# A hand-written order for the first batch's two halves in a Nyström attention and two-layer gated kernel

## The chip, the core and the metric

The kernel runs on one core of a Trainium2 chip. The metric is the device time of one execution in microseconds (us). A core has TensorE (matrix products into PSUM), VectorE, ScalarE, GpSimd and the queues that start DMA transfers; here nearly all transfers are issued from the SyncE queue (SP). In the profile's rows the engines are called PE (matmuls), PEld (its weight loads), DVE (VectorE), ACT (ScalarE), POOL (GpSimd) and SP. Each engine works through its own list of instructions in order and waits at an instruction until what it needs is there.

## The reference

Four batches of eight heads go through a Nyström attention with 32 landmarks, and the result through two gated layers. Only the first part is touched by the change:

```python
def _attn_ref(q, k, v):                       # 4 x 8 x 576 x 64
    q_lm = q.reshape(B, H, 32, 18, D).mean(axis=3)
    k_lm = k.reshape(B, H, 32, 18, D).mean(axis=3)
    A  = softmax(q    @ k_lm.T / 8)           # own scores
    Bm = softmax(q_lm @ k_lm.T / 8)
    C  = softmax(q_lm @ k.T    / 8)
    Z = Bm.T / (norm1(Bm) * norminf(Bm) + 1e-6)
    for _ in range(6):
        Z = 2 * Z - Z @ Bm @ Z
    return A @ Z @ C @ v
...
x = moe(x, silu gate); return moe2(x, sigmoid gate)   # 2304 x 512, inner width 1536
```

## The kernel before

A batch's eight heads are worked on in two halves of four heads (g = 0 and 1); names end in batch and half, so `kin0_1` holds the keys of batch 0, second half. `front(b, g)` does a half: `lm_steps("k")`, then `lm_steps("q")`, each of which sums 18 tokens into a landmark (`lm`, `ls`), transposes the landmarks (`lt`) and writes them masked into `bdk` or `bdq` on ScalarE, and turns the tokens by nine transposes in three groups (`tp`), copied by ScalarE into `kq`. Then come the landmark scores `cs` (maxima `cmx`, `nmx` on VectorE, exponentials `e` on ScalarE with their sums `csm`), the small landmark matrix `bm`, the transposed weights `et` and `eT`, their product with the values (`cv`, into `bc`), and the half's own scores `as` with maxima `amx` and exponentials `sx`. For the very first half the sum is one `tensor_reduce` and a copy on VectorE, for all other halves six additions on GpSimd (line 145 on).

`back(b)` takes both halves: it normalises `bs`, iterates the inverse in seven small products `nw`, each followed by an update `rw` on VectorE, and transposes the result to `ut` (lines 345 and 346). Between the rounds `a_steps` normalises, transposes and splits the own scores into `AH`; in batch 0 every round also issues some `warm` matmuls that compute nothing. `uw_steps` then multiplies `ut` with the first layer's weights (`pu`); the big products `pg`, `pv`, `po` follow.

Weights arrive as 64-bit floats in `raw` tiles (three of them) and are converted by `convert`: two ScalarE steps (lines 372 and 375), then two VectorE steps (377 and 381), results in `w1`, or `cv1` for the output weights, whose high and low parts `wo` are split off behind (408 on ScalarE, 409 on VectorE).

The order: the code records its work in a certain order; a scheduler below it sets each engine's list from that, and may move an instruction ahead of others where nothing forbids it. `tc.issue_after` (in the helper `behind`) holds an instruction behind a named one on its engine's list. Before the loop over words ("B0 I0 F10 U00 ...") the two halves of batch 0 run as generators that stop at the words "keys" and "weights": first half up to its weights, second half's keys, rest of the first, rest of the second. SP issues keys, queries and values of the first half, then keys and queries of the second, then a mix of later inputs and weights as buffers come free.

Of the kernel before, what the change touches and what calls it, by code (L numbers as in the profile page):

```python
# [7 lines left out]
F32 = mybir.dt.float32  # L8
# [8 lines left out]
def nystrom_moe_kernel(tc, q, k, v, wg1, wv1, wo1, wg2, wv2, wo2, out):  # L17
    nc = tc.nc
    B, H, S, D = q.shape
    M = 32  # L20
# [60 lines left out]
    def behind(what):  # L81
        return tc.issue_after(order[what].ins) if what in order else nullcontext()

    def load_attn(b, which, g):
        if which == "v":
            t = att.tile([TP, 4, R, D], F32, tag="vin", name=f"vin{b}_{g}", bufs=1)
            nc.sync.dma_start(t, v[b, 4 * g:4 * g + 4].rearrange("h (p r) d -> p h r d", r=R))
# [32 lines left out]
    def pst(b, shape, nm, g=0):  # L120

        tag = "n" if nm in ("nw", "ut") else "a"
        if b == 0:
            tag = {"tp": "gv", "cs": "o", "as": "o"}.get(nm, tag)
        return ptile(shape, tag, f"{nm}_{b}_{g}")

    def front(b, g):

        nm_ = f"{b}_{g}"

        def sm(tag, shape, bufs=2):
            return small(tag, shape, nm_, bufs)

        def lm_steps(which):
            src = inq[which, b, g]
            if (b, g) == (0, 0):
                if which == "k":
                    order["lm"] = sm("ls", [P, NU, D], 1)
                lm = order["lm"][:, 0:2] if which == "k" else order["lm"][:, 2:4]
            else:  # L140
                lm = sm("lm", [P, 2, D], 1)

            if (b, g) > (0, 0):
                x = sm("ls", [P, NU, D], 1)
                nc.gpsimd.tensor_tensor(x, src[:, 0:NU], src[:, NU:], op=ALU.add)
                nc.gpsimd.tensor_tensor(x[:, 0:4], x[:, 0:4], x[:, 4:8], op=ALU.add)
                nc.gpsimd.tensor_tensor(x[:, 0:2], x[:, 0:2], x[:, 2:4], op=ALU.add)
                nc.gpsimd.tensor_tensor(x[:, 0], x[:, 0], x[:, 8], op=ALU.add)
                for w in range(2):
                    nc.gpsimd.tensor_tensor(lm[:, w], x[:, 0], x[:, 1], op=ALU.add)  # L150
# [3 lines left out]
            yield  # L154
            bdt = sm("bd" + which, [P, 2, P], 1)

            def landmarks():
                ps = pst(b, [P, P], "lt", g)
                with behind(("tp", b, g, which)):
                    order["lt", b, g, which] = nc.tensor.transpose(ps, flat(lm), ident)  # L160
                for w in range(2):
                    nc.scalar.activation(bdt[:, w], ps, AF.Copy, scale=pmask[:, w:w + 1])


            tokens_first = (b, g) == (0, 0) or (b, g, which) == (0, 1, "k")
            if not tokens_first:
                landmarks()
                yield
            t = sm("kq", [P, NU, P])
            for i in range(3):  # L170
                ps = pst(b, [P, 3, P], "tp", g)
                for j in range(3):
                    u = 3 * i + j
                    with behind("scores" if (b, g, which) == (0, 1, "k") else None):
                        order["tp", b, g, which] = nc.tensor.transpose(ps[:, j], flat(src[:, 2 * u:2 * u + 2]), ident)  # L175
                nc.scalar.copy(t[:, 3 * i:3 * i + 3], ps)
                yield
            if tokens_first:
                landmarks()
                yield  # L180
            load_next(b, g, which)
            return bdt, t
# [833 lines left out]
```

## Time and profile before

| | us |
|---|---|
| median of three runs | 860.38 (860.14 to 862.11) |
| the profiled execution | 859.69 |
| its span in the profile | 857.9 |
| TensorE busy | 838.2 |
| VectorE busy | 661.9 |
| end of `ut`, which releases the first big product | 42.11 |

The profile is of one execution. Times in its rows count from the span's start. "Busy" of TensorE contains waits inside the pipeline. The number in brackets at the end of a row is the time that the engine stood idle just before, with what ended it.

### The profile page before, as it was taken

What the parts mean: (1) busy time and instruction counts of PE and PEld (TensorE: products, weight loads), DVE (VectorE), ACT (ScalarE), POOL (GpSimd) and SP (SyncE); (2) the same over time, 40 slices, a digit from 0 to 9 for tenths busy, and PEclk for the clock granted to TensorE, in tenths of its full rate; (3) what the DMA queues carried; (4) which work ended last, traced back from release to release, by engine and by line L of the source; (5) the groups of instructions that cost most, each with busy time, mean ns of one, the idle gap of its engine ahead of it and who ended that gap; (6) DMA issues with size and microseconds to landing.
All of it is one profiled execution on the core that took longest, in us unless ns stands there. A gap on an engine that the chain in (4) does not pass through costs nothing.

```text
span 857.9 us, 15969 instructions
## 1 busy us (share of the span) xinstructions
PE 838.2 (98%) x6214; PEld 698.8 (81%) x6214; DVE 661.9 (77%) x1298; ACT 471.0 (55%) x965; POOL 59.3 (7%) x90
## 2 busy tenths in 40 slices
PE   6899999999999999999999999999999999999997
PEld 4677777888888888889898888888888788888886
DVE  5999676866976987577889777979779985678655
ACT  5677565456652754235359655555637485455421
POOL 5634330000000000000000000000000000000000
PEclk9999999999999999999999999999999999999999
DMA  8775421021430631002117515244334552232003
GB/s 277 196 230 175 126 57 29 2 87 48 145 117 1 194 102 50 1 26 74 37 62 239 179 58 188 99 148 159 111 140 164 166 179 88 74 123 74 7 19 99
DMA packets 41677, 93.32 MB, mean 109 GB/s; under 512 B 5889, under 2 KB 9217, under 8 KB 41601
## 3 DMA queue, kind: packets, MB, share of 16 engines
q1 hardware_dynamic: 40352, 90.72, 33.1%
q10 hardware_dynamic: 1248, 1.57, 0.7%
q8 instruction: 49, 0.80, 0.4%
q14 instruction: 28, 0.22, 0.1%
HBM read 72.88 MB, written 19.40 MB: 108 GB/s over the span
## 4 chain that ended last, share of the span: by engine, by line
PE 91%; DVE 4%; ACT 2%; DMA 1%; issue 1%; POOL 0%; SPq 0%; ACTq 0%; DVEq 0%; POOLq 0%
PE po L65 36%; PE pv L65 22%; PE pg L65 22%; PE pu L65 3%; PE pvr L65 2%; PE pgr L65 2%; PE nw L65 1%; PE tp L175 1%; PE cs L65 1%; DMA kin<-in_k_dram 1%; PE as L65 1%; DVE cv L377 1%; PE et L232 1%; PE cv L65 0%; DVE AH L273 0%
## 5 line engine op out<-in xcount | busy, mean ns | idle before, releaser
L65 PE MATMUL po<-wo,h 128*128 128x512 f32 (+1 forms) x435 | 109.7, 388 | 0.0
L65 PEld LDWEIGHTS po<-h,wo 128*128 128x128 f32 x480 | 82.3, 188 | 27.9 <-issue 7.5
L65 PE MATMUL po<-h,wo 128*128 128x512 f32 (+1 forms) x480 | 103.9, 373 | 0.0
L65 PE MATMUL pg<-AH,uw 128*128 128x288 f32 x552 | 94.4, 298 | 0.6 <-ACT uw L408 0.6
L65 PEld LDWEIGHTS po<-wo,h 128*128 128x128 f32 x435 | 81.1, 188 | 16.9 <-ACT h L408 0.3
L65 PE MATMUL pv<-AH,uw 128*128 128x288 f32 x552 | 92.1, 298 | 0.9 <-DVE sg L590 0.6
L835 DVE TENSOR_TENSOR oacc<-po,oacc 128x512 f32<-128x512 f32 (+1 forms) x91 | 60.2, 678 | 34.8 <-PE po L65 34.7
L65 PEld LDWEIGHTS pg<-AH,uw 128*128 128x128 f32 x552 | 80.0, 188 | 7.1 <-issue 3.4
L65 PEld LDWEIGHTS pv<-AH,uw 128*128 128x128 f32 x552 | 78.7, 188 | 4.5 <-DVE sg L590 2.3
L372 ACT ACTIVATE cv<-raw 128x512 f32<-128x512 f32 x84 | 56.9, 679 | 28.7 <-DVE st L381 9.0
L65 PE MATMUL po<-hl,wo 128*128 128x288 f32 x384 | 66.9, 309 | 0.1
L377 DVE SCALAR_TENSOR_TENSOR cv<-cv,cv 128x512 uint32<-128x512 uint32 x84 | 59.0, 705 | 1.4 <-ACT cv L375 1.3
L65 PEld LDWEIGHTS po<-hl,wo 128*128 128x128 f32 x384 | 54.0, 188 | 6.9 <-issue 3.3
L375 ACT ACTIVATE cv<-raw 128x512 uint32<-128x512 uint32 x84 | 55.9, 673 | 5.0 <-DVE wo L409 5.0
L648 DVE TENSOR_TENSOR acc<-po,acc 128x512 f32<-128x512 f32 x64 | 43.5, 686 | 14.9 <-PE po L65 14.9
L65 PE MATMUL pg<-AH,wk 128*128 128x512 f32 x192 | 52.1, 390 | 0.0
L65 PE MATMUL pv<-AH,wk 128*128 128x512 f32 x192 | 51.5, 389 | 0.0
L593 ACT ACTIVATE sg<-pg 128x288 f32<-128x288 f32 x64 | 26.0, 406 | 42.7 <-PE pg L65 42.5
L408 ACT CAST h<-h 128x288 fp32r<-128x288 f32 x64 | 27.4, 430 | 30.5 <-DVE h L594 30.3
L409 DVE TENSOR_TENSOR h<-h,h 128x288 fp32r<-128x288 f32 x64 | 29.1, 456 | 19.0 <-ACT h L408 18.8
L65 PEld LDWEIGHTS pv<-AH,wk 128*128 128x128 f32 x192 | 36.0, 188 | 7.5
L65 PEld LDWEIGHTS pg<-AH,wk 128*128 128x128 f32 x192 | 35.7, 188 | 7.2
(208 smaller groups left out, 1721.5 us busy)
## 6 DMA issues: line engine op xcount, KB each, us to landing
raw<-in_moe_w_out_dram SPq DMA_DIRECT2D x36, 512.0 KB, 4.5
raw<-in_moe_w_gate_dram SPq DMA_DIRECT2D x48, 128.0 KB, 3.4
raw<-in_moe_w_val_dram SPq DMA_DIRECT2D x48, 128.0 KB, 3.5
raw<-in_moe_w_gate_dram SPq DMA_DIRECT2D x24, 256.0 KB, 3.0
raw<-in_moe_w_val_dram SPq DMA_DIRECT2D x24, 256.0 KB, 4.0
wkd<-st SPq DMA_DIRECT2D x24, 256.0 KB, 3.0
wtd<-tf SPq DMA_DIRECT2D x12, 512.0 KB, 3.0
st<-wkd SPq DMA_DIRECT2D x24, 256.0 KB, 3.1
```

The costliest lines, as they stand in the source:

```text
L65: return nc.tensor.matmul(o, l, r, start=start, stop=stop, skip_group_check=True)
L175: order["tp", b, g, which] = nc.tensor.transpose(ps[:, j], flat(src[:, 2 * u:2 * u + 2]), ident)
L232: nc.tensor.transpose(ps[:, j, :], flat(e[:, r // 2, r % 2]), ident)
L372: nc.scalar.activation(t0, hiw.bitcast(F32), AF.Copy, scale=2.0 ** -112)
L375: nc.scalar.activation(u1, low, AF.Copy, scale=0.875 * 2.0 ** -29, bias=0.49)
L377: nc.vector.scalar_tensor_tensor(u1, u0, 3, u1, op0=ALU.logical_shift_left, op1=ALU.bitwise_or)
L408: nc.scalar.copy(hi, x)
L409: nc.vector.tensor_tensor(lo, x, hi.bitcast(F32), op=ALU.subtract)
L593: nc.scalar.activation(sg, pss[0], AF.Silu)
L648: nc.vector.tensor_tensor(sl, ps, sl, op=ALU.add)
L835: nc.vector.tensor_tensor(acc[:, ds], ps, acc[:, ds], op=ALU.add)
```

## The change

The generators of batch 0 are replaced by a class `Front` with a method for each step and a function `first_fronts` that calls the steps of both halves in an order written out by hand. All other batches run the same steps from `Front.steps`.

- Queries are loaded ahead of keys. For the first half the query landmarks come first, then key tokens, key landmarks' sum, landmark scores, then the query tokens.
- Three of the four landmark sums of batch 0 (queries and keys of the first half, keys of the second) are five additions each on VectorE; the second half's queries stay on GpSimd.
- The first half's own scores are recorded ahead of the second half's key tokens, whose transposes are held behind them, and whose copies are held behind the exponential of `bs`.
- The weights' first two pieces are loaded ahead of the second batch's keys (`load_to(2)`), the third behind the second half's values.
- The query transposes of batch 1, half 0, are held behind the second, their landmarks behind the third round of batch 0's inverse.
- The first two ScalarE steps of the first weight piece are held behind a copy of the second half's keys.

```diff
+        def sums(self, which, eng, after=None):
+            src = inq[which, self.b, self.g]
...
+                x = self.sm("sx", [P, NU, D], 3)
+                lm = x[:, 4:6]
+            with behind(after):
+                eng.tensor_tensor(x, src[:, 0:NU], src[:, NU:], op=ALU.add)
+            eng.tensor_tensor(x[:, 0:4], x[:, 0:4], x[:, 4:8], op=ALU.add)
+            eng.tensor_tensor(x[:, 0:2], x[:, 0:2], x[:, 2:4], op=ALU.add)
+            eng.tensor_tensor(x[:, 0], x[:, 0], x[:, 8], op=ALU.add)
...
+                eng.tensor_tensor(lm, x[:, 0:1].to_broadcast([P, 2, D]), x[:, 1:2].to_broadcast([P, 2, D]), op=ALU.add)
...
-                nc.vector.tensor_reduce(lm[:, 0], src.rearrange("p u d -> p d u"), axis=AX.X, op=ALU.add)
-                nc.vector.tensor_copy(lm[:, 1], lm[:, 0])
...
+            with behind(("round", 3) if (self.b, self.g, which) == (1, 0, "q") else None):
+                nc.tensor.transpose(ps, flat(self.lm[which]), ident)
...
+    def first_fronts():
+
+        f, s = Front(0, 0), Front(0, 1)
+        load_to(2)
+        f.sums("q", nc.vector)
+        f.landmarks("q")
+        for i in range(3):
+            f.tokens("k", i)
+        f.sums("k", nc.vector)
+        for w in range(2):
+            f.scores(w)
+        f.landmarks("k")
+        for i in range(3):
+            f.tokens("q", i)
+        f.exponentials()
+        f.norm()
+        load_next(0, 0, "k")
+        s.sums("q", nc.gpsimd)
+        for i0, i1 in ((0, 5), (5, NU)):
+            f.own(i0, i1)
+        s.sums("k", nc.vector, ("shifted", 0, 0))
+        for i in range(3):
+            s.tokens("k", i, ("own", 0, 0), ("bs", 0, 0))
+        f.recip()
+        for hf in range(2):
+            f.turned(hf)
+        f.weighted()
+        load_next(0, 0, "v")
+        s.landmarks("q")
+        for w in range(2):
+            s.scores(w)
+        s.landmarks("k")
+        s.norm()
+        s.exponentials()
+        with behind(("v", 0, 1)):
+            load_to(3)
+            load_next(0, 0, "q")
+            load_next(0, 1, "k")
+        for i in range(3):
+            s.tokens("q", i)
+        load_next(0, 1, "q")
+        s.recip()
+        for hf in range(2):
+            s.turned(hf)
+        s.weighted()
+        for i0, i1 in ((0, 5), (5, NU)):
+            s.own(i0, i1)
...
-        for x in "kqv" if g == 0 else "kq":
+        for x in "qkv" if g == 0 else "qk":
             load_attn(0, x, g)
...
-    fronts = [front(0, g) for g in range(2)]
-    for g, to in ((0, "weights"), (1, "keys"), (0, None), (1, None)):
-        for said in fronts[g]:
-            if to is not None and said == to:
-                break
+    first_fronts()
...
+        if w == "I0":
+            load_next(0, 1, "v")
```

How this moves instructions on the engines' lists shows at three places. In the rows, `x0_1_331` is a tile of batch 0, half 1, with a serial number at the end, and the last figures are the output's size.

VectorE, from the first half's own scores to the second half's first maximum, before:

```order
L254 TENSOR_REDUCE amx0_0_255<-as_0_0_256 128x10
L255 TENSOR_TENSOR sx0_0_254<-as_0_0_256,amx0_0_255 128x320
L254 TENSOR_REDUCE amx0_0_255<-as_0_0_280 128x8
L255 TENSOR_TENSOR sx0_0_254<-as_0_0_280,amx0_0_255 128x256
L263 TENSOR_REDUCE asm0_0_494<-sx0_0_254 128x18
L240 TENSOR_SCALAR bc0_152<-cv_0_0_226,rc0_0_181 128x64
L264 TENSOR_SCALAR asm0_0_494<-asm0_0_494 128x18
L265 RECIPROCAL asm0_0_494<-asm0_0_494 128x18
L201 TENSOR_REDUCE cmx0_1_331<-cs_0_1_335 128x1
L267 TENSOR_TENSOR sx0_0_254<-sx0_0_254,asm0_0_494 128x576
L201 TENSOR_REDUCE cmx0_1_331<-cs_0_1_341 128x1
```

The same place after the change:

```order
L254 TENSOR_REDUCE amx0_0_205<-as0_0_0_206 128x10
L220 TENSOR_SCALAR rc0_0_272<-csm0_0_177 128x1
L255 TENSOR_TENSOR sx0_0_204<-as0_0_0_206,amx0_0_205 128x320
L254 TENSOR_REDUCE amx0_0_205<-as_0_0_230 128x8
L151 TENSOR_TENSOR sx0_1_250<-kin0_1_97 128x576
L255 TENSOR_TENSOR sx0_0_204<-as_0_0_230,amx0_0_205 128x256
L152 TENSOR_TENSOR sx0_1_250<-sx0_1_250 128x256
L221 RECIPROCAL rc0_0_272<-rc0_0_272 128x1
L372 TENSOR_SCALAR bsm0_183<-bsm0_183 128x1
L153 TENSOR_TENSOR sx0_1_250<-sx0_1_250 128x128
L154 TENSOR_TENSOR sx0_1_250<-sx0_1_250 128x64
L341 TENSOR_REDUCE asm0_0_512<-sx0_0_204 128x18
```

The sums of the second half's keys (`sx0_1_250`) now stand between the own scores' steps, and `rc0_0` ahead of them.

VectorE, the last rounds of batch 0's inverse up to the copy of `ut`, before:

```order
L336 SCALAR_TENSOR_TENSOR rw0_540<-rw0_523,nw_0_0_529 128x192
L381 SCALAR_TENSOR_TENSOR w1_0_584<-cv0_620,cv1_621 128x512
L273 TENSOR_TENSOR AH_88<-sx0_1t_580,AH_88 128x576
L336 SCALAR_TENSOR_TENSOR rw0_557<-rw0_540,nw_0_0_546 128x192
L201 TENSOR_REDUCE cmx1_0_708<-cs_1_0_712 128x1
L377 SCALAR_TENSOR_TENSOR cv1_629<-cv0_628,cv1_629 128x512
L342 SCALAR_TENSOR_TENSOR rw0_571<-rw0_557,nw_0_0_560 128x128
L381 SCALAR_TENSOR_TENSOR w1_0_584<-cv0_628,cv1_629 128x512
L346 COPY ut0_84<-ut_0_0_573 128x128
```

The same place after the change:

```order
L418 SCALAR_TENSOR_TENSOR rw0_527<-rw0_510,nw_0_0_516 128x192
L418 SCALAR_TENSOR_TENSOR rw0_541<-rw0_527,nw_0_0_530 128x192
L461 SCALAR_TENSOR_TENSOR cv1_632<-cv0_631,cv1_632 128x512
L418 SCALAR_TENSOR_TENSOR rw0_558<-rw0_541,nw_0_0_547 128x192
L465 SCALAR_TENSOR_TENSOR w1_0_602<-cv0_631,cv1_632 128x512
L461 SCALAR_TENSOR_TENSOR cv1_643<-cv0_642,cv1_643 128x512
L418 SCALAR_TENSOR_TENSOR rw0_575<-rw0_558,nw_0_0_564 128x192
L465 SCALAR_TENSOR_TENSOR cv1_643<-cv0_642,cv1_643 128x512
L424 SCALAR_TENSOR_TENSOR rw0_589<-rw0_575,nw_0_0_578 128x128
L493 TENSOR_TENSOR wo0_0_603<-cv1_643,wo0_0_603 128x512
L428 COPY ut0_84<-ut_0_0_591 128x128
```

Two conversion steps and a low part of the output weights (`cv1_643`, `wo0_0`) now stand ahead of `ut`, the maximum `cmx1_0` behind it, and two rounds follow each other directly. From nmx of the second half to the row ahead of `ut`, the list has 45 instructions before and 47 after.

TensorE, around `ut`, before:

```order
L65 MATMUL cs_1_0_712<-kq1_0_656,bdq1_0_682 32x288
L65 MATMUL nw_0_0_546<-rw0_540 32x96 x8
L65 MATMUL warm0_447<-ident_75 128x128 x2
L65 MATMUL cs_1_0_712<-kq1_0_656,bdq1_0_682 32x288 x3
L65 MATMUL cs_1_0_718<-kq1_0_656,bdq1_0_682 32x288
L65 MATMUL nw_0_0_560<-rw0_557 32x96 x8
L65 MATMUL warm0_447<-ident_75 128x128 x2
L65 MATMUL cs_1_0_718<-kq1_0_656,bdq1_0_682 32x288 x3
L345 MATMUL ut_0_0_573<-ident_75,rw0_571 128x128
L65 MATMUL warm0_447<-ident_75 128x128 x4
L65 MATMUL pu0_0_1_825<-w1_0_584,ut0_84 32x512
```

The same place after the change:

```order
L65 MATMUL nw_0_0_578<-rw0_575 32x96 x8
L65 MATMUL warm0_465<-ident_75 128x128 x2
L65 MATMUL cs_1_0_711<-kq1_0_661,bdq1_0_687 32x288
L427 MATMUL ut_0_0_591<-ident_75,rw0_589 128x128
L65 MATMUL warm0_465<-ident_75 128x128 x4
L65 MATMUL pu0_0_1_830<-w1_0_602,ut0_84 32x512
...
L65 MATMUL cs_1_0_711<-kq1_0_661,bdq1_0_687 32x288 x3
L65 MATMUL cs_1_0_717<-kq1_0_661,bdq1_0_687 32x288 x4
```

Seven of the eight landmark score products of batch 1, half 0, have moved from ahead of `ut` to behind `pu` (eight `pu` rows, of which one stands here).

## Rows read from the trace of the kernel before

**Rows 1.** The page's part 1: busy us, share of span, instructions, by engine.
```profile
PE 838.2 (98%) x6214; PEld 698.8 (81%) x6214; DVE 661.9 (77%) x1298; ACT 471.0 (55%) x965; POOL 59.3 (7%) x90
```

**Rows 2.** Stretches: length, busy us of PE, PEld, DVE, ACT, POOL; clock, DMA, GB/s.
```profile
20.00:25.00 5.00, 2.61 (x36) 1.74 (x28) 4.93 (x13) 2.96 (x10) 4.61 (x7) 0.77 1.01 285
...
30.00:35.00 5.00, 4.38 (x71) 3.52 (x61) 5.00 (x10) 3.10 (x9) 4.69 (x6) 1.00 1.04 259
...
45.00:60.00 15.00, 13.96 (x207) 12.01 (x207) 14.58 (x30) 12.20 (x32) 6.32 (x9) 1.00 0.68 204
...
72.00:80.00 8.00, 6.89 (x108) 4.63 (x105) 7.85 (x16) 4.14 (x10) 4.19 (x6) 1.00 0.44 136
...
120.00:857.00 737.00, 733.23 (x4590) 617.55 (x4580) 564.83 (x1057) 392.36 (x763) 8.93 (x14) 1.00 0.30 96
```

**Rows 3.** VectorE in time, 4 to 43: start, length, line, operation, [idle before].
```profile
4.61 2.14 DVE L152 TENSOR_REDUCE ls<-kin 128x64 f32<-128x1152 f32 x1 [3.53 <-DMA kin<-in_k_dram]
6.78 0.19 DVE L153 COPY ls<-ls 128x64 f32<-128x64 f32 x1
...
13.56 0.21 DVE L223 TENSOR_SCALAR rc<-csm 128x1 f32<-128x1 f32 x1 [1.33 <-ACT e L208]
...
17.00 0.42 DVE L254 TENSOR_REDUCE amx<-as 128x8 f32<-128x256 f32 x1
...
18.41 0.75 DVE L263 TENSOR_REDUCE asm<-sx 128x18 f32<-128x576 f32 x1 [0.53 <-ACT sx L257]
...
21.64 0.21 DVE L206 TENSOR_SCALAR nmx<-cmx 128x1 f32<-128x1 f32 x1
...
41.82 0.29 DVE L346 COPY ut<-ut 128x128 f32<-128x128 f32 x1 [0.38 <-PE ut L345]
42.02 0.45 DVE L201 TENSOR_REDUCE cmx<-cs 128x1 f32<-128x288 f32 x1
42.39 0.68 DVE L377 SCALAR_TENSOR_TENSOR cv<-cv,cv 128x512 uint32<-128x512 uint32 x1
```

**Rows 4.** TensorE in time, 4 to 24 us, same columns.
```profile
4.72 2.15 PE L175 MATMUL tp<-ident,kin 128*128 128x128 f32 x9 [4.72 <-DMA kin<-in_k_dram]
...
10.12 1.18 PE L65 MATMUL cs<-kq,bdq 128*32 128x288 f32 x16 [0.47 <-ACT bdq L162]
...
11.29 1.20 PE L175 MATMUL tp<-ident,kin 128*128 128x128 f32 x9
...
19.06 1.18 PE L65 MATMUL cs<-kq,bdq 128*32 128x288 f32 x16
...
22.69 0.45 PE L232 MATMUL et<-ident,e 128*96 128x128 f32 x1 [2.39 <-ACT e L208]
```

**Rows 5.** ScalarE in time, 8 to 45 us.
```profile
12.31 0.65 ACT L208 ACTIVATE e<-cs,nmx 128x288 f32<-128x288 f32 x1
...
13.63 0.86 ACT L176 COPY kq<-tp 128x384 f32<-128x384 f32 x2
...
17.60 0.78 ACT L257 ACTIVATE sx<-sx 128x320 f32<-128x320 f32 x2
...
19.87 0.71 ACT L372 ACTIVATE cv<-raw 128x512 f32<-128x512 f32 x1
```

**Rows 6.** VectorE in time, 20 to 34 us: operations with two operands in SBUF.
```profile
20.20 1.04 DVE L267 TENSOR_TENSOR sx<-sx,asm 128x576 f32<-128x576 f32 x1
...
22.67 1.78 DVE L381 SCALAR_TENSOR_TENSOR w<-cv,cv 128x512 uint32<-128x512 uint32 x1
...
33.38 0.74 DVE L267 TENSOR_TENSOR sx<-sx,asm 128x576 f32<-128x576 f32 x1
```

**Rows 7.** GpSimd in time: the first addition of a landmark sum.
```profile
10.07 1.42 POOL L145 TENSOR_TENSOR ls<-kin 128x576 f32<-128x576 f32 x1 [8.77 <-DMA kin<-in_k_dram]
...
22.16 1.74 POOL L145 TENSOR_TENSOR ls<-qin 128x576 f32<-128x576 f32 x1
```

**Rows 8.** TensorE in time, 33 to 42 us: one product of a round.
```profile
33.61 0.53 PE L65 MATMUL nw<-rw 32*32 32x96 f32 x16
```

More of the change, by code (lines that the diff above doesn't have):

```diff
@@ L149, in lm_steps @@
                 for w in range(2):
-                    nc.gpsimd.tensor_tensor(lm[:, w], x[:, 0], x[:, 1], op=ALU.add)
+                    eng.tensor_tensor(lm[:, w], x[:, 0], x[:, 1], op=ALU.add)
             else:
-                nc.vector.tensor_reduce(lm[:, 0], src.rearrange("p u d -> p d u"), axis=AX.X, op=ALU.add)
-                nc.vector.tensor_copy(lm[:, 1], lm[:, 0])
[L154 to L162, printed above, removed]
@@ L165, in lm_steps @@
[L165 to L177, printed above, removed]
@@ new lines, in tokens @@
+        def tokens(self, which, i, after=None, copy_after=None):
+            src = inq[which, self.b, self.g]
+            if i == 0:
+                self.t[which] = self.sm("kq", [P, NU, P])
+            ps = self.psum([P, 3, P], "tp")
+            for j in range(3):
+                u = 3 * i + j
+                with behind(after):
+                    nc.tensor.transpose(ps[:, j], flat(src[:, 2 * u:2 * u + 2]), ident)
+            with behind(copy_after):
+                order["copy", self.b, self.g, which] = nc.scalar.copy(self.t[which][:, 3 * i:3 * i + 3], ps)
@@ L257, in front, with steps @@
             nc.scalar.activation(s[:, us], s[:, us], AF.Exp)
-            yield
+        def steps(self):
+            for which in "kq":
+                self.sums(which, nc.gpsimd)
+                yield
+                self.landmarks(which)
+                yield
+                for i in range(3):
+                    self.tokens(which, i, ("round", 2) if (self.b, self.g, which) == (1, 0, "q") else None)
+                    yield
+                load_next(self.b, self.g, which)
+            for w in range(2):
+                self.scores(w)
+                yield
+            self.exponentials()
+            yield
+            self.norm()
+            self.recip()
+            yield
+            for hf in range(2):
+                self.turned(hf)
+                yield
+            self.weighted()
+            load_next(self.b, self.g, "v")
+            yield
+            for i0, i1 in ((0, 5), (5, NU)):
+                self.own(i0, i1)
+                yield
@@ L260, in a_steps, with front @@
+    def front(b, g):
+        yield from Front(b, g).steps()
     def a_steps(b, g):
@@ L359, in nystrom_moe_kernel @@
     WO = {}
+    first_convert = [("copy", 0, 1, "k")]
     def convert(t, dst):
```

172 lines of the change are left out of this document (88 added, 84 removed).

## The prediction

> **What bounds the kernel now.** The page's part on engines comes first [rows 1]: TensorE is busy 838.2 us, 98% of the span. Then the table of stretches [rows 2]: from 120 us on TensorE is busy 733.23 of 737 us, so whatever delays the first product of the big matmuls delays the end by as much, and what the change can win lies ahead of that. The same table shows who sets the pace before: in 20 to 25 us TensorE works 2.61 of 5 us and VectorE 4.93, in 30 to 35 VectorE all 5.00. So there are two pieces. Up to the second half's maximum (nmx at 21.64) the chain of landmarks and scores sets the pace and VectorE waits in places, 1.33 us at 13.56 for one [rows 3]; from there to the copy of `ut` at 41.82, VectorE does its list almost without a gap, the one wait being 0.38 us ahead of `ut` [rows 3]. The end of `ut` (42.11) releases `pu`, the first big product. I forecast when `ut` is ready after the change, and then what work is left behind it.
>
> **Sums of the first half.** Two reductions and two copies go (2.14 and 0.19 us each pair [rows 3]). Five additions per input come: 576 wide costs 0.74 beside no GpSimd work [rows 6]; 256 wide takes 0.42 in another operation [rows 3], and 128, 64 and 128 wide less; I take 1.3 for the four with the small gaps. That is 2.0 against 2.33, 0.3 us better for each input. But TensorE now begins with the queries' landmarks, which wait for their sum: it starts at 4.61 + 2.0 + 0.1 = 6.7, where before it began on keys at 4.72 [rows 4]. Its first nine transposes took 2.15 us and nine from 11.29 only 1.20: the first ones ran at the lower rate, and a start 2 us later moves that along. From 6.7: landmark 0.3, nine transposes 2.1, landmark 0.3, six transposes 1.3, so the scores begin at 10.6 or 10.7 instead of 10.12 [rows 4], and the first half's exponentials start at 13.0 instead of 12.31 [rows 5]: +0.7.
>
> **From there to the second half's scores (19.06 before [rows 4]).** The key sums leave GpSimd, which did both inputs one after the other from 10.07 [rows 7]; that gate is gone. Two others stand instead. ScalarE's list from 13.0 to the queries' landmarks: two exponentials (0.65 each), seven copies of tokens and `eT` (0.43 each, by 0.86 for two), two exponentials of own scores (0.78) and one conversion (0.71 [rows 5]) make 5.8, and with a small exponential and the first landmark factor, 0.3 to 0.4 each, 6.6: 19.6. VectorE's list: `rc`, which waits for the exponentials' sums as it did before (1.33 us of waiting [rows 3]), now stands ahead of the own scores, so VectorE stands until 14.3; then the own scores (four operations, 0.42 for the narrower ones), five additions (2.0), the 0.75 reduction [rows 3] and some small ones reach the end of `bc` at 18.9; the keys' landmark transpose waits for `bc` and the scores stand behind it. So scores at 19.6, +0.5; but the 1.04 us operation that stood between the two maxima before (the 128x576 product at 20.20 [rows 6]) is now done ahead, so nmx comes 1.8 behind the scores instead of 2.58: 21.4 against 21.64, if nothing collides.
>
> **A collision.** At 22.67 a 0.68 us operation took 1.78 [rows 6]: GpSimd's 576-wide addition had begun at 22.16 [rows 7] and the VectorE operation ended half a us behind it. There are three such holds between nmx and `ut`, about 1 us each, all of operations that read two operands from SBUF. The key sums are five of that kind, around 15.4 to 18.6. GpSimd's next addition belongs to the second batch's keys; that load is now eighth in bytes (five of 590 KB, 1.05 MB of weights, itself: 4.6 MB), and the first load had landed by 4.61 [rows 3] and the fourth by 10.07 [rows 7], so 1.77 MB took 5.46 us. At that rate, 0.32 MB per us, the eighth lands 4.0 MB or 12.4 us behind the first, near 17, inside that stretch. A hold costs 0 to 1.4 us. I take 0.7: nmx at 22.1, **+0.5** (bounds -0.5 and +1.2).
>
> The Trainium skill, "SBUF — State Buffer", section "SBUF: two separate sides", says that VectorE operations with two SBUF inputs and GpSimd's share a port pair under an exclusive lock held for the whole instruction, and section "Who interferes with whom" leaves reductions out of it on trn2. By that rule the change moves sums from an operation that can't be held to one that can, and an unlucky landing costs a whole GpSimd addition, an estimate of 1.4 us by this trace's duration; the trace agrees with the lock at all three holds, and no run here shows the additions.
>
> **VectorE's list from nmx to `ut`.** By the instruction rows of the change section, 45 operations become 47. Two conversion steps and one low part of the output weights (`cv1_643` twice, `wo0_0`), which stood behind `ut`, now stand ahead; one maximum (`cmx1_0`) goes behind it. A conversion step costs 0.68 and the maximum 0.45, a little less where neighbours overlap [rows 3]: 3 x 0.65 - 0.4 = **+1.5**. GpSimd still does three inputs in that time, so I keep the three holds.
>
> **New waits on it.** `rc` of the second half stands behind exponentials that stand behind a conversion of 0.71 on ScalarE [rows 5]: 0.45 us. And two rounds of the inverse (`rw0_527`, `rw0_541`) follow each other with nothing between; each needs a product of 0.53 us with its signals [rows 8]: 0.7 us. The wait of 0.38 for `ut` [rows 3] is covered by the low part. Together **+0.8** (bounds 0 and 1.2). Who waits: all the later rounds, then `ut`, then `pu`.
>
> **Work moved behind `ut`.** Seven of the eight score products of the second batch's first half now follow `pu`: each product is two records, 16 records took 1.18 us [rows 4], so 14 are 1.0. TensorE then waits for ScalarE's first converted `uw` anyway; I let that cover 0.4: **+0.6** (0.3 to 1.0).
>
> **Given back.** VectorE leaves the stretch with 1.5 us of work done early. TensorE's gaps behind `ut` are 15.00 - 13.96 = 1.04 in 45 to 60 and 8.00 - 6.89 = 1.11 in 72 to 80 [rows 2]; some of them VectorE causes. I take **-0.5** (from -2.2, all of them gone, to +1.5, if the second batch's rounds, which get fewer fillers on TensorE, double their gap). The loads' new order I cost at nothing: the third weight piece now waits on the queue behind the second half's values, some 18 us, but by VectorE's list it is converted only after 30, and that slack hides it; if it came 10 us late, `ut` would be as late as it.
>
> **Sum.** 0.5 + 1.5 + 0.8 + 0.6 - 0.5 = +2.9 us. The profiled execution took 859.69 with a span of 857.9; 859.69 + 2.9 = 862.6. The median of the three runs is 860.38, 0.69 above it, so I predict 860.38 + 2.9 = **863.3**.
>
> **Rivals.** First, not slower: GpSimd's sums may fall clear of VectorE's. Their landing times all change; the hold shown cost 1.78 - 0.68 = 1.1 [rows 3, 6], the three together about 3.0. Without them and without the early one (0.7) the time is 863.3 - 3.7 = 859.6. It decides if at most one of GpSimd's 576-wide additions meets a two-operand operation. For it: GpSimd is idle longer early on. Against: VectorE does such operations more than half of the time.
>
> Second, faster: VectorE isn't the pace, and TensorE's wait is. TensorE stood 2.39 us before 22.69 [rows 4], and the granted clock of 20 to 25 was 0.77 [rows 2], so part of the following work ran at 1.2 instead of 2.4 GHz: 0.23 x 2.61 = 0.6 us. In the new order the second half's own scores come ahead of its weights' transposes and fill that wait. If all of it counted: 860.38 - 2.39 - 0.6 = 857.4. Against it: VectorE was busy 4.93 of 5 in that stretch, so TensorE's speed there was not what `ut` waited for.
>
> The Trainium skill, "TensorE: Matmul & The Clock Gate", Part 1, says that an idle array falls back to the lower clock and sustained work releases it; the 0.77 agrees. By it less idling is worth time whatever the order; the second rival is what that would give here, and the first transposes, now later, are what it would cost.
>
> Third, worse: the early hold costs its whole 1.4, a fourth meets the rounds (1.0), and the second batch's rounds lose 1.5: 866 and more.
>
> **How the numbers follow.** A measurement of this kernel can tell about 0.3% from no change, 2.6 us: 857.8 to 863.0. Forecast (VectorE paces, +1 to +5): 0.60, of which 0.41 lies over 863.0 and 0.19 under. No holds: 0.20, all within. TensorE's wait: 0.13, faster. Worse: 0.07, slower. So faster 0.13, same 0.39, slower 0.48. The range 859.3 to 866.3 leaves out the second rival and the upper part of the third, under 0.2.
>
> **What would show it.** In the new profile: TensorE's first instruction near 6.7; the second half's nmx near 22 (later than 21.6); some of the 128x576, 256 and 128 wide additions of the second half's keys longer than their kind; VectorE without a gap from there to `ut` except near `rc` and between two rounds; `ut` copied near 44.6; score products of the second batch behind `pu`. A `ut` before 42 with VectorE's list as dense as before would make the prediction wrong, as would gaps of TensorE behind 45 us that shrink by more than 2 us.

## The result and the profile after

The changed kernel takes 866.01 us (864.43 to 866.85, six runs) against 860.73 us (860.14 to 862.11) for the kernel before on the same chip: a ratio of 1.0057 with a 95% interval of 1.0044 to 1.0070. It is slower, by 5.3 us where 2.9 was forecast, and inside the range. The two profiled executions, on which the sum was made, lie 6.5 us apart (859.69 and 866.18; spans 857.9 and 864.4).

Where the time went shows first in the table of stretches of the changed kernel. Columns as in [rows 2]: length, then busy us of PE, PEld, DVE, ACT, POOL, then clock, DMA share, GB/s.

```profile
20.00:25.00 5.00, 3.95 (x151) 2.98 (x140) 4.28 (x15) 4.99 (x16) 1.51 (x4) 1.00 1.03 260
25.00:30.00 5.00, 2.82 (x45) 1.92 (x33) 5.00 (x16) 3.95 (x10) 1.85 (x2) 1.00 1.04 360
30.00:35.00 5.00, 2.83 (x37) 2.06 (x37) 4.96 (x12) 1.24 (x2) 4.69 (x6) 0.70 0.99 256
35.00:40.00 5.00, 4.62 (x43) 3.44 (x44) 2.81 (x6) 1.88 (x6) 3.50 (x7) 0.50 0.45 132
40.00:45.00 5.00, 5.00 (x55) 3.66 (x53) 4.18 (x6) 3.35 (x7) 3.47 (x4) 0.78 0.84 242
...
120.00:857.00 737.00, 736.35 (x4727) 620.28 (x4727) 566.52 (x1072) 395.85 (x775) 8.94 (x14) 1.00 0.30 95
```

Two of the same stretches of the kernel before, which [rows 2] doesn't hold:

```profile
25.00:30.00 5.00, 4.54 (x142) 3.77 (x144) 4.86 (x18) 3.47 (x9) 1.57 (x6) 0.89 0.53 141
...
35.00:40.00 5.00, 4.34 (x68) 2.52 (x69) 5.00 (x9) 4.58 (x9) 4.28 (x6) 1.00 0.48 159
```

Behind 120 us TensorE is as full as before (736.35 of 737). Between 25 and 35 us it does 5.65 us of work instead of 8.92, its granted clock falls to 0.50, and in 35 to 40 VectorE, which was busy all 5.00 us there, is busy 2.81. VectorE's rows in time name what it waits for (start, length, line, operation, [idle before]):

```profile
18.00 0.99 DVE L159 TENSOR_TENSOR sx<-sx 128x128 f32<-128x128 f32 x1
...
21.31 0.22 DVE L197 TENSOR_SCALAR nmx<-cmx 128x1 f32<-128x1 f32 x1
...
28.76 1.43 DVE L345 TENSOR_TENSOR sx<-sx,asm 128x576 f32<-128x576 f32 x1
...
30.36 0.76 DVE L348 STREAM_TRANSPOSE sx_1t<-sx 128x576 f32<-128x576 f32 x1
31.05 0.12 DVE L393 RECIPROCAL rr<-rr 128x2 f32<-128x2 f32 x1
31.09 0.76 DVE L461 SCALAR_TENSOR_TENSOR cv<-cv,cv 128x512 uint32<-128x512 uint32 x1
31.77 0.34 DVE L413 TENSOR_TENSOR rw<-nw,rr 128x192 f32<-128x192 f32 x1
...
37.45 0.35 DVE L418 SCALAR_TENSOR_TENSOR rw<-rw,nw 128x192 f32<-128x192 f32 x1 [0.99 <-PE nw L65]
...
39.61 0.35 DVE L418 SCALAR_TENSOR_TENSOR rw<-rw,nw 128x192 f32<-128x192 f32 x1 [1.20 <-PE nw L65]
...
44.05 0.29 DVE L424 SCALAR_TENSOR_TENSOR rw<-rw,nw 128x128 f32<-128x128 f32 x1 [0.52 <-PE nw L65]
...
45.52 0.29 DVE L428 COPY ut<-ut 128x128 f32<-128x128 f32 x1 [0.19 <-PE ut L427]
```

And TensorE's rows in time:

```profile
6.83 0.45 PE L166 MATMUL lt<-ident,sx 128*128 128x128 f32 x1 [6.83 <-DVE sx L159]
...
19.57 1.18 PE L65 MATMUL cs<-kq,bdq 128*32 128x288 f32 x16
...
26.29 0.53 PE L65 MATMUL nw<-bc 32*32 32x96 f32 x16
...
27.30 0.82 PE L178 MATMUL tp<-ident,kin 128*128 128x128 f32 x6
32.17 0.86 PE L65 MATMUL nw<-rw 32*32 32x96 f32 x16 [4.04 <-DVE rw L413]
32.96 1.22 PE L65 MATMUL warm<-ident 128*128 128x128 f32 x4
...
41.48 0.85 PE L65 MATMUL nw<-rw 32*32 32x96 f32 x16
...
43.45 0.53 PE L65 MATMUL nw<-rw 32*32 32x96 f32 x16
43.91 0.71 PE L65 MATMUL warm<-ident 128*128 128x128 f32 x4
...
46.31 1.09 PE L65 MATMUL pu<-w,ut 64*32 64x512 f32 x16
47.33 1.17 PE L65 MATMUL cs<-kq,bdq 128*32 128x288 f32 x14
48.43 0.53 PE L65 MATMUL pg<-AH,uw 128*128 128x288 f32 x2
```

The first product, the first update and the second product in the kernel before:

```profile
27.14 0.95 PE L65 MATMUL nw<-bc 32*32 32x96 f32 x16
...
29.35 0.32 DVE L331 TENSOR_TENSOR rw<-nw,rr 128x192 f32<-128x192 f32 x1
...
29.73 0.53 PE L65 MATMUL nw<-rw 32*32 32x96 f32 x16 [0.38 <-DVE rw L331]
```

Read together: the first update of the inverse (`rw`, line 413) begins at 31.77, where it began at 29.35 before. Its inputs' chain of short steps was spread out by long ones: the second half's `sx` product (1.43 us, itself held up), its transpose (0.76) and a conversion step (0.76) stand just ahead of it. TensorE, which had already done the own scores and the next batch's key tokens, had nothing in the meantime and stood 4.04 us. When it resumed, its clock was at the lower level (0.50 of 2.4 GHz): a product of a round took 0.86 us instead of 0.53 [rows 8], the four fillers behind it 1.22 instead of 0.71, and this lasted from 32.17 to beyond 41.48, through five of the six rounds. VectorE had fewer long steps left to do between the rounds, and three times it waited for such a product (0.99, 1.20 and 0.52 us).

The stretch from the second half's nmx to `ut` as one row, before and after:

```profile
21.64:41.82 20.18, 17.39 (x307) 12.51 (x308) 19.60 (x47) 13.29 (x32) 13.73 (x18) 0.92 0.71 196
```

```profile
21.31:45.52 24.21, 18.43 (x258) 13.41 (x248) 20.34 (x48) 14.62 (x35) 13.86 (x18) 0.79 0.87 248
```

It is 4.03 us longer, of which VectorE's work is 0.74 (19.60 to 20.34) and its idle time 3.29 (0.58 to 3.87). With nmx 0.33 earlier, `ut` comes 3.70 later (41.82 to 45.52). What follows `ut`, to the end of the execution, grows from 817.87 to 820.66, by 2.79; the two make the 6.49.

### The profile page after: what moved, and what is told of

Read it like the earlier page. It is cut to its first block, busy times and chain, and to the rows that moved or that the text cites. A ratio compares the mean times of both kernels' runs of the same rounds, so it can differ in the third digit from the quotient of the medians.

```text
span 864.4 us, 15958 instructions
## 1 busy us (share of the span) xinstructions
PE 841.8 (97%) x6214; PEld 700.9 (81%) x6214; DVE 663.5 (77%) x1309; ACT 471.7 (55%) x965; POOL 55.7 (6%) x84
## 3 DMA queue, kind: packets, MB, share of 16 engines
q10 hardware_dynamic: 1248, 1.57, 0.7%
## 4 chain that ended last, share of the span: by engine, by line
PE 91%; DVE 5%; DMA 1%; ACT 1%; issue 1%; POOL 0%; DVEq 0%; SPq 0%; POOLq 0%; ACTq 0%
PE po L65 35%; PE pg L65 22%; PE pv L65 22%; PE pu L65 3%; PE pvr L65 2%; PE pgr L65 2%; PE tp L178 1%; PE nw L65 1%; PE cs L65 1%; PE as L65 1%; DMA raw<-in_moe_w_val_dram 1%; PE cv L65 1%; DVE w L465 1%; DMA qin<-in_q_dram 0%; PE et L229 0%
```

## The experiments

**Theories.** One: TensorE's empty 4 us and the low clock behind it make the rounds late. Two, a rival: it is VectorE's order, the long steps ahead of the first round, and the clock is only a companion. Three, another: one part of the hand-written front (additions, keys on VectorE, early own scores, queries first) costs it, and undoing that part brings it back. And since the second rival of the prediction said that filling TensorE's wait is worth time, that was tried in the kernel before.

All twelve runs in one table. "Ratio" is against the kernel before, measured beside it, with its 95% interval; the other columns are of the profiled execution, in us.

| kernel | median | ratio | nmx | first `rw` | `ut` | nmx to `ut` | behind `ut` |
|---|---|---|---|---|---|---|---|
| before | 860.73 | | 21.64 | 29.35 | 41.82 | 20.18 | 817.87 |
| after | 866.01 | 1.0057 [1.0044, 1.0070] | 21.31 | 31.77 | 45.52 | 24.21 | 820.66 |
| e1 gap, one filler | 864.41 | 1.0052 [1.0033, 1.0070] | 20.10 | 30.48 | 41.84 | 21.74 | 821.26 |
| e2 gap filled | 863.17 | 1.0036 [1.0019, 1.0052] | 21.96 | 32.69 | 42.67 | 20.71 | 820.47 |
| e3 before, gap filled | 860.99 | 1.0005 [0.9996, 1.0014] | 21.44 | 29.99 | 43.83 | 22.39 | 818.14 |
| e4 chain first | 861.90 | 1.0016 [1.0004, 1.0029] | 20.64 | 27.27 | 41.37 | 20.73 | 820.96 |
| e5 sums by reduction | 868.33 | 1.0086 [1.0057, 1.0115] | 23.20 | 34.17 | 47.85 | 24.65 | 820.48 |
| e6 keys on GpSimd | 865.90 | 1.0062 [1.0041, 1.0082] | 21.75 | 32.21 | 46.29 | 24.54 | 820.37 |
| e7 own scores late | 866.57 | 1.0064 [1.0041, 1.0086] | 21.64 | 33.68 | 47.10 | 25.46 | 819.52 |
| e8 keys first | 868.07 | 1.0075 [1.0046, 1.0105] | 24.38 | 37.67 | 49.79 | 25.41 | 818.54 |
| e9 before, additions | 861.56 | 0.9999 [0.9990, 1.0007] | 21.50 | 29.15 | 41.43 | 19.93 | 818.13 |
| e10 as e4, one run | 863.48 | | 21.01 | 27.52 | 42.97 | 21.96 | 820.51 |
| e11 e4, late loads | 865.68 | 1.0047 [1.0030, 1.0064] | 21.07 | 28.17 | 40.78 | 19.71 | 822.38 |
| e12 e4, late landmark | 861.15 | 1.0001 [0.9989, 1.0013] | 21.22 | 27.73 | 40.97 | 19.75 | 819.59 |

**e1 and e2: the gap alone.** Behind the last key transpose of the second batch's first half, TensorE gets fillers that compute nothing, one in e1 and twelve in e2. The two kernels have the same order otherwise, so they stand against each other; against the changed kernel a few instructions lie elsewhere.

```diff
-                    nc.tensor.transpose(ps[:, j], flat(src[:, 2 * u:2 * u + 2]), ident)
+                    last = nc.tensor.transpose(ps[:, j], flat(src[:, 2 * u:2 * u + 2]), ident)
+            if (self.b, self.g, which, i) == (1, 0, "k", 2):
+                with tc.high_priority(2000):
+                    warm(ptile([P, P], "o", "warm1"), 12, last)    # e1: 1
```

> The changed kernel with one filler product (two records) put into TensorE's 4.04 us wait ahead of the first round; the planner, seeing one more instruction there, also moves the second batch's landmark of queries up by a round and one conversion step and one low part of the output weights behind the copy of ut. It is the control for the next run, whose instruction order is the same on every engine. Clock theory (TensorE's idle time ahead of the rounds lowers its granted clock and the rounds then run at the lower level): wait still about 3.8 us, granted clock near 0.5 from 32 to 42 us, ut near 44.3, time 864.5 to 866. List theory (VectorE's longer list ahead of the first round alone makes ut late): the same time, since the list ahead of the first round is the same.

> The same instruction order as the control on every engine, with twelve filler products (24 records, about 3.3 us at the full rate) in the same place in place of one. Clock theory: granted clock 1.00 through the rounds, a round's product 0.53 us in place of 0.86, VectorE's waits of 0.5 to 1.2 us in the rounds gone, ut 2.0 to 2.7 us earlier than in the control and the time 2 us lower. List theory: ut and time as in the control within 0.3 us.

TensorE's row at the first update in e1, and two stretches of it:

```profile
30.88 0.86 PE L65 MATMUL nw<-rw 32*32 32x96 f32 x16 [3.85 <-DVE rw L416]
```

```profile
30.00:35.00 5.00, 4.12 (x44) 3.02 (x44) 4.22 (x8) 0.53 (x1) 4.68 (x6) 0.52 0.72 218
35.00:40.00 5.00, 5.00 (x80) 3.65 (x79) 2.64 (x5) 3.21 (x7) 4.53 (x8) 0.80 0.26 77
```

The same of e2:

```profile
33.09 0.53 PE L65 MATMUL nw<-rw 32*32 32x96 f32 x16 [1.27 <-DVE rw L416]
```

```profile
30.00:35.00 5.00, 3.25 (x50) 2.83 (x52) 5.00 (x11) 1.42 (x3) 4.61 (x7) 1.00 1.04 273
35.00:40.00 5.00, 4.82 (x92) 3.50 (x84) 4.04 (x8) 2.93 (x7) 4.69 (x6) 1.00 0.17 54
```

Filling the gap keeps the clock at 1.00 and the product at 0.53, and VectorE's waits for products fall from 3.1 to 0.9 us. But VectorE's work in nmx to `ut` grew from 18.53 to 19.31, by operations held up beside GpSimd (1.49 and 1.71 us where one takes 0.68), so the stretch gained 1.03 and the median 1.24 (2 us were expected), with intervals that overlap. By this pair the clock is a part, about 1 us, and not the whole: e2 is still 0.36% slower than before. But the rest doesn't lie where the second theory puts it. The stretch from nmx to `ut` in e2:

```profile
21.96:42.67 20.71, 16.94 (x284) 13.35 (x272) 19.31 (x47) 13.29 (x32) 13.10 (x16) 1.00 0.78 223
```

The first `rw` is still 10.73 us behind nmx, as against 7.71 before, and yet `ut` comes only 0.53 us later behind nmx than before (20.71 against 20.18): from the first `rw` to `ut` it takes 9.98 us instead of 12.47. What e2 still loses lies behind `ut` (820.47 against 817.87). And e1, which kept the gap and the lower clock, is at 21.74 and not at the changed kernel's 24.21: more of the 3.50 us between e2 and the changed kernel goes with the few moved instructions, or with one execution against another, than with the fillers. In e1 the lower clock also ended sooner: its products took 0.86 us from 30.88 on and 0.53 from 37.12.

**e3: the gap in the kernel before.** Eight fillers stand behind `bm` of the second half, in the wait of 2.39 us [rows 4].

```diff
+            last = mm(ps[hs], bdq[:, 0, hs], bdk[:, 0, hs])
+        if (b, g) == (0, 1):
+            with tc.high_priority(2000):
+                warm(ptile([P, P], "gv", "warm1"), 8, last)
```

> The kernel before with eight filler products (16 records, about 2.2 us) in TensorE's 2.39 us wait for the second half's exponentials; the order of every other instruction up to ut is unchanged. The rival of the prediction by which TensorE's wait and clock cost the kernel before time: granted clock of 20 to 30 us near 1.00 and 0.6 to 1.5 us less. VectorE paces the stretch: clock near 1.00 and the time unchanged within 0.5 us, ut within 0.4 us of 41.82.

Stretches of e3, and TensorE's longest wait in time:

```profile
20.00:25.00 5.00, 5.00 (x120) 4.11 (x116) 4.90 (x14) 3.58 (x12) 4.61 (x7) 1.00 0.99 277
25.00:30.00 5.00, 2.69 (x74) 2.08 (x63) 3.93 (x16) 2.32 (x5) 1.38 (x3) 0.81 0.84 209
```

```profile
27.91 0.49 PE L65 MATMUL as<-bdk,kq 128*32 128x64 f32 x10 [2.31 <-issue]
```

The stretch 20 to 25 got its clock of 1.00 (0.77 before [rows 2]) and the time did not move: 860.99 against 860.96. The profiled execution has a new wait of 2.31 us further on, with no releaser that the trace shows, so this profile says little of what the early clock would give; the eleven runs say that nothing came of it. The profile does show, in one execution, what follows a gap in the old order: behind it the clock was 0.51 in 30 to 35, a product of a round took 0.86 us at 31.45, and from the first `rw` to `ut` it took 13.84 us instead of 12.47.

**e4: the chain first.** The second half's `asm`, both transposes of `sx`, and the first VectorE step of the second to fourth converted pieces are held behind the first `rw`.

```diff
+        held = ("rw", 0) if (b, g) == (0, 1) else None
+        with behind(held):
+            nc.vector.tensor_reduce(asm, s, axis=AX.X, op=ALU.add)
...
+        with behind(("rw", 0) if b == 0 else None):
+            nc.vector.transpose(out=at, in_=flat(s))
...
+        order["rw", b] = nc.vector.tensor_tensor(RW, ps, rr[:, :, None].to_broadcast([P, 2, 96]), op=ALU.mult)
...
+        held = ("rw", 0) if 2 <= len(converted) <= 4 else None
...
+        with behind(held):
+            nc.vector.scalar_tensor_tensor(u1, u0, 3, u1, op0=ALU.logical_shift_left, op1=ALU.bitwise_or)
```

> The changed kernel with the second half's normalisation of own scores, both transposes and three conversions held on VectorE behind the first round, which is where the kernel before has most of them. Both theories want less in front of the first round; they differ in size. List theory alone: first round near 28 us in place of 31.8, TensorE's wait under 1 us, ut 1.5 to 2.5 us earlier than in the changed kernel. Clock theory on top: granted clock 1.00 in the rounds, so VectorE's waits inside them go too: ut 3.5 to 4.5 us earlier, near 41.3, and the time 861 to 863.

The first `rw` comes at 27.27, 6.63 behind nmx where the changed kernel had 10.46, and the ratio falls from 1.0057 to 1.0016: by the medians 4.1 of the 5.3 us are back (866.01 to 861.90), though the clock in 25 to 30 was 0.50 in its profile. The VectorE operations now behind the first round met GpSimd's sums there: 1.81, 1.70 and 1.21 us where their kinds take 0.68 to 0.75. The stretch from nmx to `ut`:

```profile
20.64:41.37 20.73, 18.01 (x269) 12.56 (x258) 18.51 (x44) 12.42 (x31) 15.13 (x21) 0.84 0.73 208
```

That is as long as in e2 (20.71), and the intervals of the two ratios overlap: filling TensorE ahead of the first update and clearing VectorE's long steps away from it come to the same in this stretch, and which of the two weighs more isn't shown. `ut` came 4.15 earlier than in the changed kernel, what was expected with the clock at 1.00, but 0.67 of that is an earlier nmx and the clock was at the lower level for a part.

**e5 to e8: one part of the front undone each.** e5 takes the reduction and the copy back for the first half's sums; e6 gives the second half's key sums back to GpSimd; e7 puts the first half's own scores behind the second half's key tokens; e8 loads and works the first half's keys ahead of its queries.

```diff
+            if (self.b, self.g) == (0, 0):                                   # e5
+                lm = self.lm[which] = self.sm("sx", [P, NU, D], 3)[:, 4:6]
+                nc.vector.tensor_reduce(lm[:, 0], src.rearrange("p u d -> p d u"), axis=AX.X, op=ALU.add)
+                nc.vector.tensor_copy(lm[:, 1], lm[:, 0])
+                return
...
-        s.sums("k", nc.vector, ("shifted", 0, 0))                            # e6
+        s.sums("k", nc.gpsimd)
...
+            with behind(("copy", 0, 1, "k")):                                # e7
+                f.own(i0, i1)
...
-        for x in "qkv" if g == 0 else "qk":                                  # e8
+        for x in "kqv" if g == 0 else "qk":
```

> The changed kernel with the first half's two landmark sums as one reduction and one copy each again, as in the kernel before; every other instruction stands in the same order on every engine. Sums theory (the prediction's: five additions cost 2.0 us against 2.33, 0.3 us better for each input): TensorE's first instruction 0.3 us later, the second half's nmx up to 0.6 us later, time 0 to 0.6 us above the changed kernel's 866.0. Theory of the rounds (what is lost is lost between nmx and ut): the same wait near 4 us and the same granted clock near 0.5 in the rounds, time within 1 us of 866.

> The changed kernel with the second half's key sums back on GpSimd, where they follow the query sums; five operations leave VectorE ahead of nmx and the list from nmx to ut stays as it is. Collision theory (the prediction's early hold of 0.7 us): nmx 0.5 to 1 us earlier, time 0.5 to 1 us less. Theory of the rounds: nmx may move by a microsecond, since GpSimd ends both sums near 18 us or the list of VectorE gets shorter by 2.4 us, but the wait of 4 us and the granted clock of 0.5 stay and the time stays within 1 us of 866.

> The changed kernel with the first half's own scores behind the second half's key tokens again, as in the kernel before. The planner then also moves one conversion pair ahead of the second half's own scores and starts the first round behind one more long operation. Theory of the rounds: the wait ahead of the first round is 4 us or longer, the granted clock in the rounds 0.5, time 865 to 868. Theory that the own scores' early place makes ut late (they take VectorE's time ahead of nmx): nmx 0.5 us earlier and time 1 us less.

> The changed kernel with the first half's keys loaded, transposed and summed ahead of its queries again, as in the kernel before, with the additions on VectorE. TensorE starts near 4.7 in place of 6.83. Theory of the start (the prediction's +0.7 for the first half's exponentials): first half's nmx 0.5 to 1.2 us earlier than 13.04, second half's nmx as much earlier or unchanged, time 0 to 1 us less. Theory of the rounds: the gap of 4 us and the granted clock of 0.5 stay, time within 1 us of 866.

None brings time back: 865.90 to 868.33. TensorE's wait ahead of the second product, one row each of e5, e6, e7 and e8:

```profile
34.57 0.86 PE L65 MATMUL nw<-rw 32*32 32x96 f32 x16 [4.57 <-DVE rw L418]
```

```profile
32.61 0.53 PE L65 MATMUL nw<-rw 32*32 32x96 f32 x16 [4.05 <-DVE rw L413]
```

```profile
34.08 0.86 PE L65 MATMUL nw<-rw 32*32 32x96 f32 x16 [3.72 <-DVE rw L414]
```

```profile
38.07 0.86 PE L65 MATMUL nw<-rw 32*32 32x96 f32 x16 [6.44 <-DVE rw L413]
```

All four keep the gap, a clock of 0.50 to 0.53 in 35 to 40, and 24.5 to 25.5 us from nmx to `ut`. So the third theory falls: the loss doesn't hang on any one of these parts. Two of them may be worth something in this order: without the first half's additions nmx came at 23.20, without queries first at 24.38 (21.31 with all parts; the same order gave 20.10 to 21.96 in other executions), and both medians are some 2 us above the changed kernel's, more than was expected, with intervals that overlap its own. In e5 the first half's sixteen score records took 2.13 us (1.57 in the changed kernel, 1.18 in e1), and one of the second half's key additions met GpSimd's sum as well, so not all of the 1.9 is the reduction's own:

```profile
17.77 1.38 DVE L158 TENSOR_TENSOR sx<-sx 128x128 f32<-128x128 f32 x1
```

**e9: the additions alone, in the kernel before.** Five additions in place of each of the first half's reductions and copies, nothing else.

> The kernel before with one part of the change alone: the first half's two sums as five additions each, every other instruction in the same order on every engine. Sums theory: keys' sum ends at 6.6 in place of 6.97 and the queries' at 8.6 in place of 9.2, so the first half's scores start up to 0.4 us earlier; but the second half's landmarks wait for GpSimd until 17.8, so the time is 0 to 0.4 us less, within the measurement. If the additions are worth as much here as the run with reductions showed in the changed kernel (about 2 us), the time falls to 859.

No change (0.9999), with nmx at 21.50: in that order the second half's chain doesn't wait for the first half's sums by these tenths of a microsecond.

**e10 to e12: what e4 still lacks.** Whatever its label says, the kernel of e10 is that of e4, run once more. e11 is e4 with the second batch's next loads of keys and queries moved behind the first weights word, so that GpSimd's sums of them start behind the rounds; e12 is e4 with the landmark transpose of batch 1's queries held behind the fifth round instead of the third.

```diff
-            load_next(0, 1, "k")                                             # e11
...
-        load_next(0, 1, "q")
...
         if w == "I0":
-            load_next(0, 1, "v")
+            for x in "vkq":
+                load_next(0, 1, x)
...
-            with behind(("round", 3) if (self.b, self.g, which) == (1, 0, "q") else None):     # e12
+            with behind(("round", 5) if (self.b, self.g, which) == (1, 0, "q") else None):
```

> The changed kernel with the work held behind the first round, once more for a second profile, to tell what its clock does in the rounds from one execution to another. Clock theory: where the granted clock stays at 1.00 the time from nmx to ut is 1 to 1.5 us shorter than the 20.73 us of the first profile, in which it stood at 0.50 from 25 to 30 us.

> The changed kernel with the work held behind the first round and, on top, the second batch's second half loaded two weight pieces later, so that GpSimd's sums of it no longer fall into the rounds; VectorE's list up to ut gains one maximum. Collision theory: the two-operand operations of 1.0 to 1.8 us between 32 and 41 us (0.68 or 0.75 without GpSimd) lose 2 us in all, ut comes 1.5 to 2 us earlier than in the run without this and the time falls to 860. If the collisions are covered by other waits of the rounds: time unchanged near 862.

> The changed kernel with the work held behind the first round and, on top, the second batch's landmark of queries on TensorE behind the fifth product of the rounds in place of the third; three of its score products then go behind pu again. In the second profile of the held kernel that landmark waited 2.26 us for GpSimd's sum of a load that landed at 28.3, with the rounds queued behind it. Theory that the change's early order is as good as the old one once the rounds don't wait: time 860 to 861.5, equal to the kernel before. Theory that the loss behind ut (second batch's rounds, moved score products) stays: ut 41 to 42 but time 862 to 863.

TensorE in time in e10:

```profile
32.94 0.47 PE L166 MATMUL lt<-ident,lm 128*128 128x128 f32 x1 [2.26 <-POOL lm L157]
33.56 0.86 PE L65 MATMUL nw<-rw 32*32 32x96 f32 x16
```

The landmark transpose stood in TensorE's list ahead of a round's product and waited 2.26 us for GpSimd's sum of a load that had landed at 28.30; the rounds stood behind it, and VectorE waited 2.05 us for the product. That product and the next two ran at 0.85 to 0.86 us, and though the clock was 1.00 in 25 to 30, nmx to `ut` took 21.96 us, longer than in e4 and not shorter as was expected. With the landmark behind the fifth round (e12) no loss is left to see: 861.15 against 861.07, ratio 1.0001. What this last step is worth isn't settled: e12's interval overlaps e4's, and in e4's own profile the landmark didn't wait. The stretch from nmx to `ut` in e12:

```profile
21.22:40.97 19.75, 16.99 (x272) 12.47 (x261) 18.36 (x44) 12.38 (x31) 14.08 (x19) 0.91 0.75 216
```

VectorE idles 1.39 us in it instead of 3.87, and `ut` comes 0.85 ahead of the kernel before; 1.72 more behind `ut` than before takes that back. e11, expected at 860, cleared the holds from the rounds (the longest left is 1.03 us; 19.71 from nmx to `ut`), and lost it behind `ut` (822.38): TensorE was busy 8.13 of 12 us in 72 to 84, where the kernel before had 10.89. That the later landmark sums cause this was not tried apart. No version here beat the kernel before.

**What follows.** The hand-written front can be had without loss: e12 has all of it for batch 0 and equals the kernel before, within 0.13%. In the changed kernel 3.70 of the 6.49 us between the profiles are lost up to `ut` and 2.79 behind it. Up to `ut` two things come together in the order that the scheduler made: long VectorE steps ahead of the first round, and TensorE's gap with the lower clock, which these steps bring about. Taking away either (e4; e2, with the moved instructions of e1) leaves 20.7 of 24.21 us from nmx to `ut`, so the first two theories describe one loss from two sides, and their shares stay open. A landmark of a late load ahead of a round adds to it in one execution (e10). The parts aren't additive: e4 and e12 change the gap, the clock and the holds at once. For the part behind `ut` no run shows the cause.

## Why the prediction came out as it did

| term | forecast (bounds) | measured |
|---|---|---|
| nmx of the second half | +0.5 (-0.5 to 1.2) | -0.33 |
| VectorE's list to `ut` | +1.5 | +0.74 |
| new waits on it | +0.8 (0 to 1.2) | +3.29 |
| behind `ut`, both terms | +0.1 (-1.9 to +2.5) | +2.79 |
| sum | +2.9 | +6.49 (medians: +5.3) |

Two rows came out about 0.8 us below the forecast and two 2.5 and 2.7 above it. That 866.01 lies inside the range, 0.3 us under its end, is in part luck: the forecast's own mechanism, a longer VectorE list, gave 0.74 of the 6.49.

**The front** was read rightly: TensorE's first instruction at 6.83 (6.7 forecast), the second half's scores at 19.57 (19.6), nmx 1.74 behind them (1.8). The early collision happened with the very price taken: the last key addition took 0.99 instead of 0.29, while GpSimd's 576-wide sum ran.

```profile
17.42 1.42 POOL L151 TENSOR_TENSOR ls<-kin 128x576 f32<-128x576 f32 x1 [3.52 <-DMA kin<-in_k_dram]
```

The load that started it had been forecast for "near 17". nmx was nonetheless 0.8 earlier than forecast: ScalarE's gate came 0.3 earlier (19.31 instead of 19.6), and the sum charged the 0.7 on top of that gate, while the hold lies on VectorE's, beside it. One row each of ScalarE and TensorE:

```profile
18.67 0.64 ACT L168 ACTIVATE bdq<-lt,pmask 128x128 f32<-128x128 f32 x2
```

```profile
19.31 0.33 PE L166 MATMUL lt<-ident,sx 128*128 128x128 f32 x1 [0.61 <-DVE bc L239]
```

ScalarE's factors were ready at 19.31; VectorE's held list let the scores begin at 19.57. So the hold cost 0.26 of its 0.7 there.

The Trainium skill, "SBUF — State Buffer", section "SBUF: two separate sides", tells of the exclusive lock of a port pair, and the 0.99 us addition agrees with it.

**VectorE's list** has the three added steps, and the holds are of the size assumed (3.4 us above their kinds, as before). The short operations, though, came out cheaper by some tenths, such as 0.17 for the `asm` addition that took 0.43.

**The step that failed is the new waits.** The bound of 1.2 was made from one pair of rounds that follow each other and a product of 0.53 us [rows 8], a figure that holds at full clock only. The prediction took TensorE's speed as something that `ut` doesn't wait for; in the kernel before, a clock of 1.00 in 20 to 25 moved nothing (e3). After the change it isn't so: the first product comes 0.85 earlier (26.29 against 27.14) and the first update 2.42 later, TensorE has no more work between them than before (1.36 us behind the first product against 1.32), and the waits at 37.45, 39.61 and 44.05, 2.71 us together, all end on a product. The forecast `rc` wait of 0.45 wasn't there; 0.63 for `amx` was. VectorE's order could have told it: it was read for how many instructions stand ahead of `ut`, not for how many long ones stand ahead of the first update, and the rows shown of it begin behind that place.

The Trainium skill, "TensorE: Matmul & The Clock Gate", Part 1, says that an idle array falls back to the lower clock and that sustained work releases it. The fall agrees with the trace, 4.04 us of idling and then 0.50; the release agrees less plainly: TensorE was busy 4.62 of 5 us in 35 to 40, and the product at 41.48 still took 0.85 us.

**Behind `ut`** the part that was forecast happened: 14 score records stand behind `pu`, 1.17 us, but the wait for the first converted `uw` covered more of them than assumed, and from `pu` to `pg` it takes 2.12 us instead of 2.96. What was mis-sized is "given back". The upper bound named it (the second batch's rounds get fewer fillers): in 72 to 84 us, before and after,

```profile
72.00:84.00 12.00, 10.89 (x149) 7.92 (x145) 11.85 (x24) 7.91 (x20) 7.39 (x10) 1.00 0.45 141
```

```profile
72.00:84.00 12.00, 9.96 (x217) 6.17 (x205) 11.74 (x26) 9.42 (x22) 8.39 (x11) 1.00 0.73 184
```

TensorE is busy 0.93 us less in the same window, and 1.23 less (9.66 against 10.89 of 12 us) when each is counted from the first product of the second batch's rounds, at 69.57 and 74.05. From the first `pg` to the first `pg` of the third batch it is 2.60 longer, 1.66 of it busy and 0.94 idle. Of the busy part 0.80 are the second batch's `bm` and first `et` products, which lay ahead of the first `pg` before and lie behind it now; the rest has no name. From there to TensorE's last product it is 0.33 longer and the end behind that 0.7, both unexplained.

**Open.** How the loss up to `ut` splits between VectorE's order and the clock isn't known. The same instructions up to nmx gave it at 20.10 to 21.96 in different executions, which single profiles can't average out. Why the stretch behind `ut` is 2.5 to 3.4 us longer in most of the variants isn't settled, though it is clear of chance: the three profiles with the order of before (before, e3, e9) have 817.87 to 818.14 there. e7, e8 and e12 have less of it (1.65, 0.67 and 1.72), e11 more (4.51), and e4 as much as the changed kernel.

## What to carry to other kernels

When early work is pulled forward, look at the place that it left as well: which engine has nothing there now, and whose long operations the scheduler has slipped into the chain of short ones. A list without gaps on the engine that sets the pace is no proof of a good order, since work done ahead of a latency chain is missing as cover behind it; hold such work behind the first link of the chain (e4), or keep the other engine busy up to there (e2). And keep a product that needs a late load out of a list that a latency chain shares (e10, e12).

## What the runs showed of the hardware

- A gap of 4.04 us on TensorE was followed by some 10 us at half the clock, though the engine was busy most of that time; a product of a round took 0.86 instead of 0.53 us. In e1 a gap of 3.85 us was followed by some 6 us of it.
- An addition of only 128x128 on VectorE can take 1.38 us instead of 0.29 beside a sum on GpSimd (e5): the price is that of the other engine's operation, not its own.
- One order gave nmx 1.9 us apart between executions (20.10 in e1, 21.96 in e2), while the median of the kernel before lay between 860.05 and 861.40 each time.
